# A forward and backward pass in one kernel: the forward tiles of the GLU stage one step earlier, the first weight gradients inside its last tiles

## The chip, the cores and the metric

The kernel runs on one core of a Trainium2 chip. A core has a matrix engine (TensorE, PE in the profile; its weight loads are the row PEld), VectorE (DVE), ScalarE (ACT), GpSimd (POOL) and SyncE (SP). Each engine runs its own instructions in program order and waits on semaphores for the others. Transfers are issued here by SP and GpSimd and carried by 16 DMA engines. The metric is the device time of one execution in microseconds, lower is better; runs of the kernel before: median 537.85 us of 11, from 533.74 to 543.94.

## What is computed

The reference is a residual block and its gradients with respect to nine inputs. S = 2048 rows, D = 512 columns, F = 1376 hidden columns, all bf16.

```python
def _B_ref(x, w_gate, w_up, w_down):
    g = jnp.einsum("bsd,df->bsf", x, w_gate)
    u = jnp.einsum("bsd,df->bsf", x, w_up)
    h = _sigmoid(g) * u
    return jnp.einsum("bsf,fd->bsd", h, w_down)

x = A_q
xn = _layernorm(x, axis=-1)
s = _A_ref(xn, A_k, A_v, A_shift_k, A_ssm_k, A_ssm_D)
g = _silu(_B_ref(xn, B_w_gate, B_w_up, B_w_down))
return x + s * g
```

`_A_ref` is a short shift convolution of k, a product with v, a convolution over the whole sequence length by FFT, and a product with q (here `xn`). The kernel returns the output and the gradients: of x, k, v, the shift weights, the long filter, its skip weight, and the three GLU weights.

## The kernel before

The kernel does not issue its instructions as it is written. Python generators ("streams") record operations in a list; `run_streams` picks the next stream by its progress against a share; `Rec.order` then sorts all recorded operations into one order per engine, by its own cost estimates, looking at most 700 operations ahead; `Rec.emit` (L512) issues them. That is why every row of the profile names L512, and why every tile is called `slab` or `psum`: SBUF is one slab that `Arena` and `Ring` cut up. A record of the trace is assigned to a function by counting: an engine runs in program order, and the counts agree engine by engine (5417 weight loads in the trace, 5033 matmuls and 384 transposes in the program), so the n-th record is the n-th operation.

The work has three stages. **A** (to about 155 us): FFT of k and of k*v for four channel groups (`strK`, `strV`, `strX`), and beside it the forward of nine of the 16 row tiles (`f_gen`, tiles in `FA`), one tile being 128 rows. **B**, the GLU stage (about 155 to 360 us), `stepB`: for each row tile i

- `f_gen(t)`: 88 matmuls of 128 columns for g and u of a later tile, sigma = sigmoid(g) and h = sigma*u, written to DRAM in feature-major order (`hF_d`); for the first NSP = 6 tiles of `FA`, h and sigma are loaded again by `f_ld`;
- `z_gen(i)`: 11 matmuls of 512 columns, z = h w_down, then a chain on VectorE and ScalarE to `dzA`, the gradient of z, which needs `go` (the tile of `grad_out`, loaded by `b_ld` on GpSimd's queue); `dzA` is transposed by DMA for tiles 1 to 12 and on PE for the others;
- `d_gen(i)`: 44 matmuls of 128 columns for dh, and on VectorE the gradients of u and g (`duT`, `dgT`), stored to `uF_d`, `gF_d` on SP's queue;
- `x_gen(i)`: 22 matmuls of 512 columns with `wuT` and `wgT` (weights transposed by DMA on SP's queue), then the layernorm backward on VectorE and a store.

**C** (to the end): the backward FFT (`frontC`, `backC`) mixed with the weight gradients `dW`: nine jobs, three of h (35 blocks of 16 matmuls in all with those of g and u), each needing its operand as a block `L` of 16 KB per partition, loaded from `hF_d`, `gF_d` or `uF_d` by `ld_L` as four DMA transposes of 512 KB on SP's queue. `dW` and `x_gen`, `z_gen` share two accumulator banks of PSUM.

Which tile is where: `SEQ` is the forward order 15, 13, 11, 9, 7, 5, 0, 1, 2, 3, 4, 6, 8, 10, 12, 14 and `POS[i]` a tile's place in it. In `stepB` (L1215 on) the forward of tile i + LAG (LAG = 3) runs inside step i, so that of tile 14 ends in step 11; the flag `fwd` is set there. The layernormed tile is turned by `f_xt`: on PE for places 0 and 1, by DMA on SP's queue from place 2 on. `sig_r`, `h_r` are rings of four buffers in stage B, `v_r[0]` (the third factor of the gradient of g) of three.

After `fwd` the rings of the forward weights are freed and a first block for `L` is made, after `z15` (z of tile 15 recorded) a second; only then is `ld_L` called, and it loads two jobs at most before the end of B. `dW` is run beside the rest of B with the share 0.9 to 1.8, B itself with an estimated length of 520000:

```python
live = run_streams([(gated(stepB(), "B"), 520000, 0.0, 1.0)], until=lambda: "fwd" in flags)
...
live = run_streams(live + [(dW(), 35 * 8192, 0.9, 1.8)], until=lambda: "B" in flags)
```

A stream's position is start + (end - start) * done / length; the stream that is least far goes next. In C `backC` runs from -0.05 to 0.66 against what is left of `dW` (0 to 1).

Of the kernel before, what the change touches and what calls it, by code (L numbers as in the profile page):

```python
# [23 lines left out]
NJ = 16  # L24
NFB = 11
# [4 lines left out]
LAG = 3  # L30
# [4 lines left out]
FA = [15, 13, 11, 9, 7, 5, 0, 1, 2]  # L35
NSP = len(FA) - LAG
SEQ = FA + [i for i in range(NJ) if i not in FA]
POS = {i: n for n, i in enumerate(SEQ)}
# [54 lines left out]
class Ring:  # L93
# [9 lines left out]
    def next(self):  # L103
        a = self.aps[self.i % len(self.aps)]
        self.i += 1
        return a
# [409 lines left out]
def run_streams(streams, until=None):  # L516

    live = [list(st) + [0.0] * (5 - len(st)) for st in streams]
    while live:
        if until is not None and until():  # L520
            break
        for st in sorted(live, key=lambda s: s[2] + (s[3] - s[2]) * s[4] / s[1]):
            try:
                c = next(st[0])
            except StopIteration:
                live.remove(st)
                break
            if c:
                st[4] += c
                break  # L530
        else:
            raise RuntimeError("all streams blocked")
    return live
# [91 lines left out]
def kernel_impl(ctx, tc, A_q, A_k, A_v, A_shift_k, A_ssm_k, A_ssm_D, B_x, B_w_gate, B_w_up, B_w_down,  # L625
# [15 lines left out]
    ar = Arena(slab, SLAB)  # L641
# [4 lines left out]
    def ps_mm(shape, dt=f32, name=None):  # L646
        return nc.ps(PS["mm"], shape, dt)
# [4 lines left out]
    def ps_tr(shape, dt=bf16, name=None):  # L652
        return nc.ps("tr", shape, dt)
# [19 lines left out]
    sig_r, h_r = Ring(ar, [NFB, 128], n=LAG), Ring(ar, [NFB, 128], n=LAG)  # L673
# [6 lines left out]
    flags = set()  # L680
    v_r = []

    def f_major(eng, dst, c, i, src):
        eng.dma_start(dst[c][i // 4, :, i % 4].rearrange("p (a t) -> p a t", t=128), src)

    def f_x(i):
        T[i]["xq"] = xq_r.next()
        nc.gpsimd.dma_start(T[i]["xq"], qC[:, i, :])
# [17 lines left out]
        nc.scalar.activation(xnA[:, i, :], xj, ACT.Identity, bias=nmr_all[:, i:i + 1], scale=rstd_all[:, i:i + 1])  # L706

    def f_xt(i):
        if POS[i] > 1:
            T[i]["xnT"] = xnT_r.next()  # L710
            nc.sync.dma_start_transpose(T[i]["xnT"], xnA[:, i, :])
            return
        pt = ps_tr([4, 128], name="ps_xnT")
        for db in range(4):
            nc.tensor.transpose(pt[:, db, :], xnA[:, i, db * 128:(db + 1) * 128], ident)
        T[i]["xnT"] = xnT_r.next()
        nc.evac(T[i]["xnT"], pt[:], 512)

    def f_gen(i):
        xnT = T[i]["xnT"]  # L720
        n = POS[i]
        if n + 4 < NJ:
            f_x(SEQ[n + 4])
        sigT, hT = sig_r.next(), h_r.next()
        T[i]["sig"], T[i]["h"] = sigT, hT
        uT = None if PS["wide"] else v_r[0].next()
        T[i]["v"] = uT
        for pi, (f0, nb) in enumerate(FBS):
            if PS["wide"]:
                ps = ps_mm([2, 4, 128], name="psGU")  # L730
                pg, pu = ps[:, 0], ps[:, 1]
            else:
                pg, pu = ps_mm([4, 128], name="psG")[:], ps_mm([4, 128], name="psU")[:]
            for pt_, w in ((pg, wg), (pu, wu)):
                for b in range(nb):
                    for db in range(4):
                        nc.tensor.matmul(pt_[:, b, :], w[:, db, (f0 + b) * 128:(f0 + b + 1) * 128], xnT[:, db, :],
                                         start=(db == 0), stop=(db == 3))
            nc.scalar.activation(sigT[:, f0:f0 + nb, :], pg[:, 0:nb, :], ACT.Sigmoid)
            if uT is None:  # L740
                nc.vector.tensor_tensor(hT[:, f0:f0 + nb, :], pu[:, 0:nb, :], sigT[:, f0:f0 + nb, :], ALU.mult)
            else:
                nc.evac(uT[:, f0:f0 + nb, :], pu[:, 0:nb, :], nb * 128)
            if pi == 1 and n + 2 < NJ:
                f_ln(SEQ[n + 2])
            if pi == (2 if n == 0 else 0) and n + 1 < NJ:
                f_xt(SEQ[n + 1])
            yield nb * 1024
        if uT is not None:
            nc.vector.tensor_tensor(hT, uT, sigT, ALU.mult)  # L750
            nc.vector.tensor_tensor(uT, uT, hT, ALU.subtract)
        for c, (f0, nb) in enumerate(FBS):
            f_major(nc.gpsimd, hF_d, c, i, hT[:, f0:f0 + nb])
        if n < NSP:
            nc.gpsimd.dma_start(sF_d[n].rearrange("p (a t) -> p a t", t=128), sigT)

    def f_ld(i):
        n = POS[i]
        sigT, hT = sig_r.next(), h_r.next()
        T[i]["sig"], T[i]["h"] = sigT, hT  # L760
        for c, (f0, nb) in enumerate(FBS):
            nc.gpsimd.dma_start(hT[:, f0:f0 + nb], hF_d[c][i // 4, :, i % 4].rearrange("p (a t) -> p a t", t=128))
        nc.gpsimd.dma_start(sigT, sF_d[n].rearrange("p (a t) -> p a t", t=128))
# [314 lines left out]
    dh_r = Ring(ar, [4, 128], n=2)  # L1078
    wd, wdT, wgT, wuT = wd_r.ap, wdT_r.ap, wgT_r.ap, wuT_r.ap
    dg_r, du_r = Ring(ar, [NFB, 128], n=2), Ring(ar, [NFB, 128], n=2)  # L1080

    def b_ld(i):
        T[i]["x"], T[i]["go"] = xq2_r.next(), go_r.next()
# [115 lines left out]
    def stepB():  # L1199
        f = f_gen(3)  # L1200
        yield from w_gen()
        z = z_gen(0)
        for g in (f, z, f, z, f, z, f):
            c = next(g, None)
            if c:
                yield c
        for i in range(NJ):
            f = f_gen(i + LAG) if 0 < i < NJ - LAG and i + LAG not in FA else iter(())
            d, x = d_gen(i), x_gen(i)
            z = z_gen(i + 1) if i + 1 < NJ else iter(())  # L1210

            def take(g, n):
                for _ in range(n):
                    c = next(g, None)
                    if c is None:  # L1215
                        return
                    yield c
            yield from take(d, 1)
            yield from take(f, 1)
            yield from take(z, 9)  # L1220
            if i == NJ - 2:
                flags.add("z15")
            if i + 2 < NJ:
                b_ld(i + 2)
            if i + LAG in FA[:NSP]:
                f_ld(i + LAG)
            for _ in range(3):
                yield from take(d, 1)
                yield from take(f, 1)
            yield from take(d, 9)  # L1230
            yield from take(f, 9)
            yield from take(x, 9)
            if i + LAG == SEQ[-1]:
                flags.add("fwd")

    stC = {}
    jobs = [(s, c) for s in range(3) for c in range(3)]
    srcs = (hF_d, gF_d, uF_d)
    CH = [(0, 512), (512, 512), (1024, 352)]
    Lfree = []  # L1240

    def ld_L():
        while Lfree and stC.setdefault("Ln", 0) < (len(jobs) if "B" in flags else 2):
            n, blk = stC["Ln"], Lfree.pop(0)
            stC["Ln"] = n + 1
            s, c = jobs[n]
            f0, w = CH[c]
            nb = -(-w // 128)
            L0 = blk.ap.rearrange("p a b -> p (a b)")[:, 0:NJ * nb * 128].rearrange("p (a b) -> p a b", b=128)
            for q in range(4):  # L1250
                nc.sync.dma_start_transpose(L0[:, 4 * q * nb:4 * (q + 1) * nb, :], srcs[s][c][q].rearrange("p j f -> p (j f)"))
            blk.L0 = L0
            stC["L", n] = blk
# [39 lines left out]
    def frontC():  # L1293
        for cg in range(NG):
            Qg = Qg_r.next()
            yield from step1T(lambda j: y2A[:, j, cg * GW:(cg + 1) * GW], Qg, cg in (1, 3))
            while stC["nY"] < 4 * cg:
                yield 0
            Qf = stC["Qf", cg] = Qf_r.next()
            flipT(Qg, cg in (1, 3), Qf, cg > 1)  # L1300
# [104 lines left out]
    def gated(g, flag):  # L1405
        yield from g
        flags.add(flag)
    live = run_streams([(gated(stepB(), "B"), 520000, 0.0, 1.0)], until=lambda: "fwd" in flags)
    for r in (wg_r, wu_r, xq_r, xnT_r):
        r.free()  # L1410
    Lfree.append(Ring(ar, [NJ, 512]))
    ot_r = Ring(ar, [512], n=3)
    live = run_streams(live, until=lambda: "z15" in flags)
    for r in [wd_r] + list(zw.values()):
        r.free()
    Lfree.append(Ring(ar, [NJ, 512]))
    ld_L()
    live = run_streams(live + [(dW(), 35 * 8192, 0.9, 1.8)], until=lambda: "B" in flags)
    for r in [wdT_r, wgT_r, wuT_r, sig_r, h_r, xq2_r, go_r, dg_r, du_r, wq_r, dh_r,
              dxa_r, dzT_r, dxn_r, u1_r, v_r[0]]:  # L1420
        r.free()
# [23 lines left out]
    for n in range(3):  # L1445
# [1 line left out]
    nc.sync.dma_start(Ci.rearrange("p c j n -> p (c j n)"), Ci_d[:])  # L1447
    ld_L()
    dw = live[0]
    live = run_streams([(dw[0], dw[1] - dw[4], 0.0, 1.0), (frontC(), 4 * 4096, -0.05, 0.5),  # L1450
                        (gated(backC(), "back"), 4 * 34816, -0.05, 0.66)], until=lambda: "back" in flags)
    for r in (KK_r, Qg_r, B2_r, Qf_r, Xc_r, Xw_r, P_r):
        r.free()
    Lfree.append(Ring(ar, [NJ, 512]))
# [63 lines left out]
```

## Time and profile before

| | |
|---|---|
| median of 11 runs | 537.85 us |
| the profiled execution | 538.61 us, of which span 536.8 us |
| PE busy | 497.4 us (93%), 5355 matmul records |
| VectorE busy | 401.9 us (75%) |
| ScalarE busy | 343.3 us (64%) |
| GpSimd busy | 125.3 us (23%) |
| DMA | 113.59 MB, mean 212 GB/s |
| granted clock | 0.986 on average; 0.50 at 43.6 to 50.4, 145.95 to 149.37, 326.86 to 330.27 us |

The page's second part shows the last two of these dips in the row of the clock, which is in slices of 13.4 us; the first line is the share of each slice that PE is busy, in tenths:

```profile
PE   4797899999898999999999997999999999999997
...
PEclk9997999999999999999999998999999999999999
```

A matmul's busy time contains the time to its end, so that neighbours overlap; the pace of PE is read as stretch over count. Times in the timeline are microseconds from the span's start; "[3.12 <-X]" is idle time ahead of an instruction and what ended it. A row with SPq or POOLq is an issue on that engine's queue.

### The profile page before, as it was taken

To read this page: it belongs to the slowest core of one execution; us is meant where nothing else is said; L and a number is where in the kernel's file an instruction comes from. 1 tells how busy PE (TensorE), PEld (TensorE's weight loads), DVE (VectorE), ACT (ScalarE), POOL (GpSimd) and SP (SyncE) were. 2 spreads that over 40 slices of the span, in tenths; PEclk is the share of its full clock that TensorE was granted. 3 is DMA by queue.
4 is the path that set the end of the run, shared out by engine and by line. 5 is a ranking of instruction groups with operands and counts; after the bars stand their busy time and mean duration, and the time that the engine had idled before them with its cause. 6 is when DMAs were issued, how large, how long until landed. Compare 5 with 4: busy or idle time off the path is not lost. (4 is left out here: it accounts for less than half of the span.)

```text
span 536.8 us, 13480 instructions
## 1 busy us (share of the span) xinstructions
PE 497.4 (93%) x5355; PEld 354.9 (66%) x5417; DVE 401.9 (75%) x774; ACT 343.3 (64%) x455; POOL 125.3 (23%) x241
## 2 busy tenths in 40 slices
PE   4797899999898999999999997999999999999997
PEld 2687787898786665677666655655746755676644
DVE  7859899965677799787999887767468487765831
ACT  6899999999853443354444533339857869785511
POOL 5152533445413335242424231000000000000000
PEclk9997999999999999999999998999999999999999
DMA  8977797878999465663649599998999789999953
GB/s 261 251 230 252 214 340 212 262 244 242 197 222 180 150 206 146 181 183 117 191 128 232 114 175 209 245 280 239 241 251 202 210 242 213 278 210 242 197 161 115
DMA packets 175345, 113.59 MB, mean 212 GB/s; under 512 B 116119, under 2 KB 159793, under 8 KB 175026
## 3 DMA queue, kind: packets, MB, share of 16 engines
q1 hardware_dynamic: 163648, 78.83, 61.4%
q0 software_dynamic: 11104, 33.89, 21.4%
q8 instruction: 42, 0.69, 0.6%
q14 instruction: 21, 0.17, 0.1%
q10 hardware_dynamic: 530, 0.01, 0.1%
HBM read 37.65 MB, written 45.72 MB: 155 GB/s over the span
## 5 line engine op out<-in xcount | busy, mean ns | idle before, releaser
L512 PE MATMUL psum<-slab 128*128 128x128 bf16 (+4 forms) x5355 | 497.4, 255 | 35.6 <-ACT slab L512 13.0
L512 PEld LDWEIGHTS <-slab 128*128 128x128 bf16 (+2 forms) x5417 | 354.9, 100 | 177.7 <-DVE slab L512 23.7
L512 DVE TENSOR_TENSOR slab<-slab 128x512 bf16<-128x512 bf16 (+5 forms) x472 | 270.0, 609 | 59.2 <-ACT slab L512 31.5
L512 ACT CAST slab<-psum 128x1024 bf16<-128x1024 f32 (+4 forms) x273 | 221.8, 857 | 108.4 <-PE psum L512 87.1
L512 ACT ACTIVATE slab<-psum 128x512 bf16<-128x512 f32 (+2 forms) x80 | 55.0, 690 | 47.4 <-PE psum L512 45.0
L512 ACT COPY slab<-psum 128x1024 bf16<-128x1024 bf16 (+1 forms) x46 | 45.0, 1019 | 17.9 <-PE psum L512 17.9
L512 ACT ACTIVATE slab<-slab 128x512 bf16<-128x512 bf16 (+2 forms) x53 | 41.8, 798 | 14.7 <-DVE slab L512 14.1
L512 POOL DMA_DIRECT2D out_dram<-slab x32 | 17.7, 552 | 105.0 <-DVE slab L512 105.0
L512 DVE TENSOR_TENSOR slab<-psum,slab 128x512 bf16<-128x512 f32 (+2 forms) x47 | 29.3, 626 | 11.2 <-ACT slab L512 6.5
L512 POOL DMA_DIRECT2D hF_d<-slab x48 | 26.4, 552 | 34.0 <-DVE slab L512 33.3
L512 DVE CAST slab<-psum 128x1024 bf16<-128x1024 f32 (+2 forms) x21 | 23.9, 1139 | 13.5 <-PE psum L512 10.0
L512 DVE SCALAR_TENSOR_TENSOR slab<-slab 128x512 bf16<-128x512 bf16 (+2 forms) x64 | 28.1, 439 | 6.9 <-POOL slab L512 5.7
L512 POOL MEMSET slab<- 128x128 bf16 (+3 forms) x11 | 4.3, 400 | 115.1 <-PE psum L512 114.8
L512 DVE SCALAR_TENSOR_TENSOR slab<-psum,slab 128x512 bf16<-128x512 f32 x16 | 11.0, 689 | 20.8 <-PE psum L512 20.7
L512 POOL DMA_DIRECT2D slab<-in_A_q_dram x29 | 16.2, 558 | 33.1 <-ACT slab L512 18.3
L512 POOL DMA_DIRECT2D KK_d<-slab x32 | 17.5, 548 | 22.2 <-ACT slab L512 19.3
L512 DVE TENSOR_SCALAR slab<-slab 128x1 f32<-128x1 f32 (+9 forms) x54 | 16.5, 326 | 2.1 <-ACT slab L512 1.2
L512 DVE STREAM_TRANSPOSE slab<-slab 128x1024 f32<-128x1024 f32 x8 | 14.2, 1821 | 4.6 <-ACT slab L512 4.6
L512 DVE BATCH_NORM_STATS2 slab<-slab 128x6 f32<-128x512 bf16 x16 | 11.0, 688 | 1.5 <-DMA slab<-in_A_q_dram 1.5
L512 POOL TENSOR_TENSOR slab<-slab 128x1 f32<-128x1 f32 x16 | 9.9, 616 | 9.5 <-DVE slab L512 9.3
L512 POOL DMA_DIRECT2D slab<-in_grad_out_dram x16 | 8.9, 559 | 11.8 <-DMA out_dram<-slab 7.3
L512 POOL DMA_DIRECT2D slab<-hF_d x18 | 9.7, 541 | 5.5 <-PE psum L512 4.3
(20 smaller groups left out, 32.7 us busy)
## 6 DMA issues: line engine op xcount, KB each, us to landing
KK_d<-slab POOLq DMA_DIRECT2D x32, 256.0 KB, 4.1
slab<-KK_d SPq DMA_DIRECT2D x16, 512.0 KB, 4.9
slab<-in_A_v_dram SPq DMA_DIRECT2D x4, 1024.0 KB, 10.5
hF_d<-slab POOLq DMA_DIRECT2D x32, 128.0 KB, 4.0
slab<-slab SPq DMA_DIRECT2D x32, 128.0 KB, 4.8
out_dram<-slab POOLq DMA_DIRECT2D x32, 128.0 KB, 3.0
uF_d<-slab SPq DMA_DIRECT2D x32, 128.0 KB, 2.8
gF_d<-slab SPq DMA_DIRECT2D x32, 128.0 KB, 3.2
```

Source lines behind the costliest of these rows:

```text
L512: getattr(getattr(self.nc, eng), meth)(*[place(v) for v in a], **{x: place(v) for x, v in k.items()})
```

## The change

1. In `stepB` the forward of tile i + LAG + 1 runs inside step i, from i = 0 on, so that of tile 14 ends in step 10, where `fwd` is now set. The reload of stored tiles (`f_ld`) moves behind the tile's `d_gen`.
2. `sig_r`, `h_r` and `v_r[0]` get one more buffer each.
3. Tiles 3, 4 and 6 (places 9 to 11) are turned on PE with a copy out of PSUM, no longer by DMA.
4. `ld_L` is called right after `fwd`, into the first block, and may load three jobs before the end of B.
5. B's length is given as 447000; `dW` beside it has the share 0.92 to 2.2. With the old length B's position ended below 0.9, with the new one it reaches 1.0.
6. In C, `frontC` goes to 0.44 (was 0.5) and `backC` to 0.58 (was 0.66).

```diff
@@ f_xt
-        if POS[i] > 1:
+        if POS[i] > 1 and not 8 < POS[i] < 12:
@@ rings of stage B
     dg_r, du_r = Ring(ar, [NFB, 128], n=2), Ring(ar, [NFB, 128], n=2)
+    for r in (sig_r, h_r, v_r[0]):
+        r.extend(Ring(ar, [NFB, 128]))
@@ stepB
         for i in range(NJ):
-            f = f_gen(i + LAG) if 0 < i < NJ - LAG and i + LAG not in FA else iter(())
+            f = f_gen(i + LAG + 1) if i + LAG + 1 < NJ and i + LAG + 1 not in FA else iter(())
...
-            if i + LAG in FA[:NSP]:
-                f_ld(i + LAG)
             for _ in range(3):
                 yield from take(d, 1)
                 yield from take(f, 1)
             yield from take(d, 9)
+            if i + LAG in FA[:NSP]:
+                f_ld(i + LAG)
             yield from take(f, 9)
             yield from take(x, 9)
-            if i + LAG == SEQ[-1]:
+            if i + LAG + 1 == SEQ[-1]:
                 flags.add("fwd")
@@ ld_L
-        while Lfree and stC.setdefault("Ln", 0) < (len(jobs) if "B" in flags else 2):
+        while Lfree and stC.setdefault("Ln", 0) < (len(jobs) if "B" in flags else 3):
@@ stages
-    live = run_streams([(gated(stepB(), "B"), 520000, 0.0, 1.0)], until=lambda: "fwd" in flags)
+    live = run_streams([(gated(stepB(), "B"), 447000, 0.0, 1.0)], until=lambda: "fwd" in flags)
...
     ot_r = Ring(ar, [512], n=3)
+    ld_L()
     live = run_streams(live, until=lambda: "z15" in flags)
...
-    live = run_streams(live + [(dW(), 35 * 8192, 0.9, 1.8)], until=lambda: "B" in flags)
+    live = run_streams(live + [(dW(), 35 * 8192, 0.92, 2.2)], until=lambda: "B" in flags)
...
-    live = run_streams([(dw[0], dw[1] - dw[4], 0.0, 1.0), (frontC(), 4 * 4096, -0.05, 0.5),
-                        (gated(backC(), "back"), 4 * 34816, -0.05, 0.66)], until=lambda: "back" in flags)
+    live = run_streams([(dw[0], dw[1] - dw[4], 0.0, 1.0), (frontC(), 4 * 4096, -0.05, 0.44),
+                        (gated(backC(), "back"), 4 * 34816, -0.05, 0.58)], until=lambda: "back" in flags)
```

## The prediction

> **What bounds the kernel now.** I read the busy table first: TensorE (PE) is busy 497.4 us of 536.8, so only its idle time and its slow-clock time can be won. Then I cut the span by stage (columns: stretch, length, busy us and instruction count of PE, weight loads, VectorE, ScalarE, GpSimd, then granted clock, DMA share, GB/s).
>
> ```profile
> 137.00:172.60 35.60, 30.63 (x408) 25.90 (x409) 26.09 (x55) 21.44 (x32) 8.47 (x17) 0.95 1.13 207
> 172.60:240.00 67.40, 66.20 (x632) 43.43 (x641) 57.33 (x145) 27.13 (x50) 26.78 (x49) 1.00 0.61 169
> 240.00:300.00 60.00, 59.45 (x593) 40.16 (x599) 51.54 (x130) 24.81 (x45) 19.34 (x36) 1.00 0.63 175
> 300.00:318.00 18.00, 17.80 (x183) 12.28 (x183) 17.28 (x43) 10.44 (x18) 4.90 (x9) 1.00 0.80 132
> 318.00:334.00 16.00, 12.28 (x92) 7.88 (x92) 12.02 (x32) 5.06 (x11) 3.33 (x8) 0.89 0.95 179
> 360.00:510.00 150.00, 145.51 (x1493) 94.53 (x1513) 103.39 (x136) 113.18 (x127) 1.77 (x4) 1.00 0.98 231
> ```
>
> In the GLU stage (about 160 to 360) PE is full except in two places: 5.0 us before 172.6, and 3.7 us after 318, where the clock is also down. VectorE is close behind (17.28 of 18.00 before the hole). The timeline shows what the holes are:
>
> ```profile
> 172.60 5.77 PE L512 MATMUL psum<-slab 128*128 128x512 bf16 x25 [1.85 <-DMA slab<-in_B_w_up_dram]
> ...
> 310.06 0.54 POOL L512 DMA_DIRECT2D slab<-in_grad_out_dram  x1
> ...
> 314.90 11.09 SPq L512 DMA_TRANSPOSE slab<-hF_d  x1
> 323.89 0.42 DVE L512 TENSOR_TENSOR slab<-slab 128x512 bf16<-128x512 bf16 x1 [3.12 <-DMA slab<-in_grad_out_dram]
> 326.42 3.50 PEld L512 LDWEIGHTS <-slab 128*128 128x128 bf16 x37 [3.50 <-DVE slab L512]
> ```
>
> and, cut as above, the stretch behind the last hole:
>
> ```profile
> 326.90:330.30 3.40, 3.18 (x31) 3.12 (x30) 3.30 (x11) 2.02 (x4) 1.08 (x2) 0.50 1.13 282
> ```
>
> At 170.4 PE reaches `x_gen(0)` and waits 2.2 us (1.85 after the weight load) for the last transposed `wuT`. At 310.06 GpSimd issues the load of `go` of tile 14; it releases VectorE only at 323.89, 13.8 us later, while SP's queue spends 11.09 us on the fourth transposed load of h. VectorE stands 3.12 us, the dz chain takes another 2.53 us to the PE transposes at 326.42, PE stands 3.5 us there, of which I count 3.4, and then runs 3.18 us of work at clock 0.50, which costs half of it, 1.6. A third hole (2.5 us at 143.8, SP's swap of the k spectrum) keeps its place and its queue order, and is left alone.
>
> **Edit 1: forward tiles one step earlier.** In the changed order `x_gen(0)` is the 2133rd PE operation, before it was the 2086th. 47 more operations stand ahead of the wait; their price comes from a stretch of 128-column work and one of 512-column work:
>
> ```profile
> 190.80:194.00 3.20, 3.20 (x57) 3.08 (x56) 2.99 (x9) 2.79 (x6) 0.54 (x1) 1.00 0.90 330
> 509.30:522.90 13.60, 13.55 (x64) 6.18 (x64) 4.77 (x4) 2.34 (x4) 0.00 (x0) 1.00 0.57 179
> ```
>
> 3.20/57 = 0.056 us and 13.60/64 = 0.213 us (0.216 below, with the change of tile). So 47 x 0.056 = 2.6 us of work that PE does anyhow now hides the 2.2 us. Bounds: 0 to -2.2. I take -2.2: even if the weights land as late as now, the cover is longer than the wait, and three DMA transposes of x leave SP's queue ahead of or among them. With each tile its three h stores and one load of x move ahead on GpSimd's queue; they keep their number, and the loads of `go` they are moved past are due 10 us later or more. The fifth buffer of sigma and h and the fourth of v only permit the order; they cost no instruction.
>
> **Edit 2: tiles 3, 4 and 6 are turned on PE.** 12 more PE operations, 12 x 0.056 = +0.7 us; three more copies out of PSUM (ScalarE 128x512, 0.59 us each) hide in 137 to 172.6, where ScalarE is busy 21.44 of 35.6; uncovered they would be 1.8. Taken: +0.7; bounds 0.7 to 2.5. No row isolates a transpose; the nearest is the 0.056 of 128-column matmuls, and that pace is what I use. The Trainium skill speaks against it ("TensorE: Matmul & The Clock Gate", Part 4: PE-mode transpose): about 275 ns for a 128x128 transpose within a kernel, by which the term would be +3.3 us and the forecast 535.2.
>
> **Edit 3: what the order does to VectorE.** This is the price. With the f tiles gone earlier, tiles 9 to 13 run without them, and a tile of d, x and z alone has more VectorE than PE work. I counted both between the end of one `x_gen` (which releases VectorE's first `x` operation) and the matmul that needs the last of it, with these rows (busy over count):
>
> ```profile
> L512 DVE TENSOR_TENSOR slab<-slab 128x512 bf16<-128x512 bf16 x240 | 93.4, 422 | 8.7 <-DMA slab<-in_grad_out_dram 3.5
> L512 DVE TENSOR_TENSOR slab<-psum,slab 128x512 bf16<-128x512 f32 x34 | 23.3, 686 | 8.7 <-PE psum L512 4.6 <-ACT slab L512 4.1
> L512 DVE SCALAR_TENSOR_TENSOR slab<-slab 128x512 bf16<-128x512 bf16 x32 | 23.0, 720 | 0.6
> L512 DVE TENSOR_TENSOR slab<-slab 128x1408 bf16<-128x1408 bf16 x23 | 20.4, 889 | 1.0 <-ACT slab L512 0.6
> ```
>
> Changed order, `x_gen(8)` to the wait in `x_gen(12)`: 58 products of 512 at 0.389 (22.6), 4 from PSUM at 0.686 (2.7), 6 of 384 at 10.6/32 = 0.33 (2.0), 4 of 1408 at 0.887 (3.5), 2 scalings of 1408 at 4.8/9 = 0.53 (1.1), 12 x-form operations (8 at 0.72, 4 at 0.69: 8.5), 4 small ones at 0.16 and 8 accumulator reads at 0.08 (1.3): 41.7 us. PE in between: 115 of 512 columns at 0.216, 216 of 128 at 0.056, 8 of 256 at 0.11: 37.8. VectorE is 3.9 over. At the front, `x_gen(1)` to `x_gen(4)`, the same count gives 33.8 against 32.6: 1.2 over. Checked on the order before: `x_gen(0)` to `x_gen(4)` 45.5 against 43.2, 2.3 over, where PE really stood 0.40 + 1.12 = 1.5; `x_gen(10)` to `x_gen(12)` 20.6 against 19.6, 1.0 over, where it stood 0.46 + 0.87 = 1.3. The count errs by about +0.25 on average, so I expect 5.1 - 0.5 = 4.6 us. It replaces 1.5 + 1.3 and 0.5 at `x_gen(10)`, 3.3 us. Taken: +1.3; bounds 0 (the elastic case) to +3.
>
> **Edit 4: h's transposed loads from the moment the f tiles end.** The four loads of block 0 move ahead: the fourth now stands with the start of `x_gen(10)`, not in `x_gen(11)`, and the four of block 1 stay in tile 13. So the stall at tile 14 goes (-3.4) with its half clock (-1.6): -5.0, bounds -5.0 to +8 (below). What is late next is `go` of tile 13: its slot is freed by the store of tile 9's output. In the changed order there are 15.4 us of PE work from that store to the dz transposes of tile 13 (56 operations of 512 columns, 51 others); 2.5 of it is the dz chain, so store plus load may take 12.9. The DMA table's medians are 3.0 (stores to `out_dram`) and 4.2 (loads of `grad_out`), 7.2 together. Before, the cover was 19.2 and store plus load took 303.81 to 323.89, 20.1: 20.1 + 2.5 - 19.2 = 3.4, which is the hole. On SP the second and third load of h stand on both sides of the dz transpose of tile 10, which has 7.5 us until `d_gen(10)`; the rows before are 2.06 and 3.93 us, so it holds. Behind the fourth: the dz transpose of tile 12 and the stores of d(11); dz of 12 has 8.3 us until `d_gen(12)`, enough for a 4 us load and not quite for an 11 us one.
>
> **Edit 5: dW of h between tiles 14 and 15, a third load before the end of B, new shares for C.** Same matmuls, other order: 48 instead of 32 of them before `x_gen(15)` ends or right behind it, 94 instead of 133 after the last of `backC`. In C, PE's waits are short (all in 360 to 510 are below 1 us each, 4.5 us idle together). The PE work between a `step3T` and the `inv3` that needs it is 4.0 to 13.5 us before and 3.4 to 11.2 after; waits appeared where it was below about 5. ScalarE, the fuller of the others (113.18 of 150), does not get ahead of PE in either order. Taken: 0; bounds -1.5 to +2.
>
> **Sum.** -2.2 + 0.7 + 1.3 - 5.0 + 0 = -5.2 us. The profiled execution took 538.61 us (536.8 of span, 1.8 around it), 0.8 above the median of the runs, 537.85; I put the sum on the median: 537.85 - 5.2 = 532.6.
>
> **The rivals.** *VectorE takes over.* For: 51.54 of 60 and 17.28 of 18 busy. If the 5.1 us stand without the 0.5, and two of these waits pull the clock to 0.50 for a window as at 145.95 and 326.9 (1.6 each): 532.6 + 0.5 + 3.2 = 536.3, within 0.5%. Against: the waits come as pieces of about 1 us, and the 2.2 us at 170.4 left the clock at 1.00. Against that in turn: 2.5 us of idle at 143.76 were followed by 0.50. The Trainium skill ("TensorE: Matmul & The Clock Gate", Part 1: The HAM clock gate) asks for a whole idle window of about 3.4 us before the clock falls, by which this rival would be 533.1.
>
> *The stuck load moves to tile 13 (slower).* Place: GpSimd's queue behind SP's fourth transposed load of h. If store plus load take 20.1 us again, PE stands 20.1 + 2.5 - 15.4 = 7.2 us, plus 1.6 of clock: 541.4. It decides from 12.9 us on; from about 16 us the gain is gone, from 19.3 the kernel is slower. For: the cover is 3.8 us shorter, since no f tile stands there, and 352 KB of sigma for tile 13 are issued just ahead. Against: only one load of h (512 KB) falls there, where before three and h's own stores came within 12 us; beside the one at 284.34 the loads landed in 6 us.
>
> *The wait at `x_gen(0)` only shifts* (the weights land later, as f's stores now share the queues): 534.8.
>
> **How the numbers follow.** Forecast 0.56, VectorE 0.15, stuck load 0.20 (two thirds of it slower), shifted wait 0.09 (half each side of the bound). About 0.5%, 2.7 us, is what a measurement can tell from no change. Faster 0.61, same 0.25, slower 0.14. Range: -1.5 of C and -1.3 of VectorE below the forecast give 529.8, taken as 529.5; upward to 540, which leaves the full stuck load out.
>
> **What would show it.** Right: no PE wait on `in_B_w_up` before the first `x_gen`; no VectorE wait over 1 us on `in_grad_out` after 250; clock 1.00 from 150 to the end; several PE waits of 0.5 to 1.5 us on VectorE in the last third of the GLU stage; the first 512-column runs of dW before the last `x_gen`. Wrong: a VectorE wait on a load in tiles 12 to 15, a second 0.50 window, or PE idle in C well above 4.5 us.

## The result, and the profile after

The changed kernel takes 530.62 us (median of 12 runs, 526.02 to 542.31), the kernel before 536.98 (47 runs beside it): ratio 0.9882, 95% interval 0.985 to 0.9915. In two later sets of runs the same kernel stood at 0.9912 (0.9873 to 0.9952) and 0.9885 (0.983 to 0.994). Forecast were 532.6 and a range of 529.5 to 540.

The first profiled execution of the changed kernel took 537.48 us (span 535.7), 6.9 above the median of its runs; two more profiles stand below. Its busy times and clock by stretch (columns as before: stretch, length, busy us and count of PE, weight loads, VectorE, ScalarE, GpSimd, granted clock, DMA share, GB/s):

```profile
168.30:172.70 4.40, 0.51 (x3) 0.04 (x2) 4.33 (x10) 0.28 (x1) 2.14 (x4) 1.00 1.21 237
172.90:176.30 3.40, 3.40 (x9) 1.19 (x8) 1.00 (x4) 0.00 (x0) 1.44 (x3) 0.50 0.97 288
...
300.00:318.00 18.00, 16.92 (x149) 10.68 (x150) 17.27 (x45) 6.13 (x10) 4.62 (x11) 1.00 0.72 173
318.00:334.00 16.00, 15.56 (x115) 8.74 (x116) 15.23 (x41) 7.22 (x13) 2.16 (x4) 1.00 0.59 174
...
360.00:510.00 150.00, 144.31 (x1427) 93.96 (x1445) 103.76 (x125) 110.54 (x122) 1.77 (x4) 0.99 0.95 220
```

The hole at tile 14 is filled (15.56 of 16.00 where it was 12.28), and 300 to 318 has become a stretch in which PE waits a little for VectorE (16.92 of 18.00, it was 17.80; VectorE 17.27). But a hole that the prediction had closed is there and larger: of the 4.4 us ahead of 172.7 PE is busy 0.51, and what follows runs at clock 0.50 for 3.4 us. The timeline of the same execution:

```profile
165.33 4.12 SPq L512 DMA_TRANSPOSE slab<-in_B_w_up_dram  x2
...
172.71 5.52 PE L512 MATMUL psum<-slab 128*128 128x512 bf16 x17 [3.90 <-DMA slab<-in_B_w_up_dram]
...
289.73 8.62 PEld L512 LDWEIGHTS <-slab 128*128 128x128 bf16 x75 [1.26 <-DVE slab L512]
...
298.61 0.54 POOL L512 DMA_DIRECT2D out_dram<-slab  x1 [3.56 <-DVE slab L512]
...
300.59 3.79 SPq L512 DMA_TRANSPOSE slab<-hF_d  x1
302.44 0.54 POOL L512 DMA_DIRECT2D slab<-in_grad_out_dram  x1
...
315.22 0.54 POOL L512 DMA_DIRECT2D slab<-in_grad_out_dram  x1
...
489.91 6.26 PE L512 MATMUL psum<-slab 128*128 128x128 bf16 x45 [2.16 <-ACT slab L512]
```

The wait at `x_gen(0)` is still for the last `wuT`. The store of tile 9's output (298.61) and the load of `go` of tile 13 behind it (302.44) now stand beside SP's fourth load of h (300.59); the load landed at 308.2, and no VectorE instruction waits for `grad_out` any more. The last line is new: a wait in C of 2.16 us by this row, 2.49 from one weight load to the next, again with a half-clock window behind it.

### The profile page after: what moved, and what is told of

Same layout as the page of the kernel before. It is cut to its first block, busy times and chain, and to the rows that moved or that the text cites. A ratio compares the mean times of both kernels' runs of the same rounds, so it can differ in the third digit from the quotient of the medians.

```text
span 535.7 us, 13494 instructions
## 1 busy us (share of the span) xinstructions
PE 497.4 (93%) x5373; PEld 353.5 (66%) x5429; DVE 404.0 (75%) x777; ACT 342.7 (64%) x455; POOL 124.5 (23%) x241
## 4 chain that ended last, share of the span: by engine, by line
PE 52%; DVE 20%; ACT 12%; issue 7%; DMA 4%; SPq 3%; POOL 1%; DVEq 0%; ACTq 0%; POOLq 0%
PE psum L512 52%; DVE slab L512 20%; ACT slab L512 12%; SPq L512 3%; DMA slab<-in_A_q_dram 1%; DMA out_dram<-slab 1%; DMA slab<-in_B_w_up_dram 1%; DMA sF_d<-slab 1%; POOL KK_d L512 0%; POOL slab L512 0%; POOL hF_d L512 0%; POOL ksh_d L512 0%; DVEq L512 0%; ACTq L512 0%; POOLq L512 0%
## 5 line engine op out<-in xcount | busy, mean ns | idle before, releaser
L512 DVE TENSOR_TENSOR slab<-slab 128x512 bf16<-128x512 bf16 (+6 forms) x472 | 268.7, 608 | 50.1 <-ACT slab L512 28.5
L512 ACT CAST slab<-psum 128x1024 bf16<-128x1024 f32 (+3 forms) x270 | 219.7, 860 | 99.1 <-PE psum L512 72.2
L512 ACT COPY slab<-psum 128x1024 bf16<-128x1024 bf16 (+1 forms) x49 | 47.2, 1003 | 13.8 <-PE psum L512 13.8
L512 DVE CAST slab<-psum 128x1024 bf16<-128x1024 f32 (+2 forms) x24 | 27.0, 1126 | 18.7 <-PE psum L512 15.2
L512 POOL DMA_DIRECT2D hF_d<-slab x48 | 26.1, 547 | 30.7 <-DVE slab L512 30.5
```

What stands on the lines that cost most here:

```text
L512: getattr(getattr(self.nc, eng), meth)(*[place(v) for v in a], **{x: place(v) for x, v in k.items()})
```

## The experiments

To compare executions I took, for every weight load, the interval to the next one less the pace of its width at full clock (0.056 us for 128 columns, 0.216 for 512, others in proportion). What is left is time that PE lost to waits and to half clock. Summed by stretch, one profiled execution per row ("before" or "changed" says which PE order the row has in front of C; "at `x_gen(0)`" is the wait and the first few matmuls behind it, so that the rest of a half-clock window falls in the next column; the last column is from the last weight load to the end of the span):

| execution | order | start to 143 | to `x_gen(0)` | at `x_gen(0)` | to `x_gen(8)` | to end of `x_gen(12)` | to end of `x_gen(15)` | C | last load to end | span |
|---|---|---|---|---|---|---|---|---|---|---|
| before | before | 31.9 | 4.4 | 2.0 | 0.8 | 0.9 | 4.7 | 7.1 | 4.3 | 536.8 |
| b_look | before | 31.6 | 3.4 | 2.5 | 2.5 | 0.8 | 1.0 | 7.0 | 4.3 | 533.9 |
| b_early_loads | before | 30.5 | 0.4 | 2.8 | 0.8 | 0.9 | 2.3 | 8.0 | 4.3 | 530.6 |
| b_new_C | before | 30.4 | 0.4 | 3.3 | 2.4 | 0.8 | 1.0 | 7.5 | 4.3 | 531.1 |
| after | changed | 31.7 | 0.2 | 4.5 | 1.3 | 2.7 | -0.1 | 9.1 | 4.9 | 535.7 |
| a_again | changed | 32.6 | 0.1 | 3.5 | 1.0 | 2.7 | -0.1 | 5.6 | 4.7 | 531.6 |
| a_third | changed | 30.1 | 0.1 | 3.6 | 1.2 | 2.7 | -0.1 | 6.9 | 4.4 | 530.4 |
| a_old_C | changed | 31.6 | 0.6 | 1.4 | 0.0 | 2.7 | -0.1 | 5.5 | 7.2 | 530.3 |
| a_old_C_pool | changed | 32.8 | 0.2 | 2.4 | 1.7 | 2.7 | -0.1 | 6.0 | 3.7 | 530.9 |
| a_late_loads | changed | 30.5 | 0.1 | 0.0 | 0.0 | 4.8 | -0.1 | 7.0 | 4.6 | 528.4 |
| a_edits123 | changed | 31.9 | 0.1 | 0.7 | 0.0 | 3.3 | -0.1 | 9.6 | 4.0 | 531.0 |
| a_dma_turn | edit 2 undone | 31.4 | 1.9 | 0.3 | 0.0 | 2.7 | -0.1 | 6.7 | 4.3 | 528.0 |
| a_swap0 | gate first | 31.1 | 1.3 | 0.0 | 0.0 | 2.7 | -0.1 | 5.6 | 4.1 | 526.2 |
| a_swap_pool | gate first | 30.5 | 0.1 | 0.0 | 0.4 | 2.7 | -0.1 | 6.0 | 3.7 | 524.8 |

Some columns repeat to 0.1 us in every execution of one order (to the ends of `x_gen(12)` and `x_gen(15)` after the change): these are waits that the order makes, most of them for VectorE. Others differ from one execution to the next of the same order: these are waits for transfers.

The two columns between `x_gen(8)` and the end of `x_gen(15)` have to be read together, since one kind of wait changes its column with the order. A matmul in the first step of the backward FFT waits for a copy by ScalarE, which itself stands behind VectorE:

```profile
308.78 11.27 PE L512 MATMUL psum<-slab 128*128 128x256 bf16 x88 [0.97 <-ACT slab L512]
308.79 0.85 PEld L512 LDWEIGHTS <-slab 128*128 128x128 bf16 x6 [1.25 <-issue]
```

This is the first profile of the change; the wait, 1.2 us, comes before the end of `x_gen(12)`. In b_look, b_early_loads and b_new_C another matmul of the same step waits 1.2, 1.7 and 1.2 us behind that end. Both columns together are 5.6, 1.8, 3.2 and 1.8 us in the order before and 2.6 in the three profiles of the changed kernel.

### a_again, a_third, b_look: the same two kernels, profiled again

No edit.

> The changed kernel once more, for a second profile of it. The first showed three things that the prediction did not have: the hole at 143.8 gone, the wait at x_gen(0) not hidden but grown to 4.25 us with a half-clock window behind it, and a new wait of 2.5 us at 487 in C, also with a half-clock window. Theory 1: all three belong to the change; then they stand here again at the same places (x_gen(0) at least 3 us, 487 at least 2 us) and the profiled execution is again near 537. Theory 2: the wait at x_gen(0) belongs to the change (PE comes earlier by the hole of 143.8, the weights do not), but its size and the wait at 487 depend on how the transfers fall in that execution; then x_gen(0) shows 2 to 4 us, 487 less than 1 us, and the profile is near 531.

> The changed kernel unchanged, to stand beside the other three on the same chip, and for a third profile: x_gen(0) waits 1 to 4.5 us (two profiles had 4.25 and 3.11), no hole at 143.8, no wait of VectorE over 1 us on grad_out after 250, and no wait over 1.5 us in C if that of 2.5 us at 487 was of that one execution.

> The kernel before once more, for a second profile. The first showed a hole of 2.5 us at 143.8 and the stall of 3.4 us at tile 14, each with a half-clock window; the kernel with the early call alone, whose PE, VectorE and ScalarE orders are those of the kernel before, showed neither and yet had the same median. Theory 1 (both belong to the kernel before): both stand here again, span near 535. Theory 2 (both depend on how the transfers fall in one execution): at least one of them is missing or under 1 us, and other waits stand in their place (VectorE at x_gen(13) and in C).

Measured: a_again 529.56 us, ratio 0.9912 (0.9873 to 0.9952); a_third 530.64, ratio 0.9885 (0.983 to 0.994); b_look 535.67, one run. The wait at `x_gen(0)` is there in both new profiles of the change, 3.11 and 3.30 us. That of a_again (the same view, in the same columns):

```profile
172.40 5.83 PE L512 MATMUL psum<-slab 128*128 128x512 bf16 x19 [2.76 <-DMA slab<-in_B_w_up_dram]
```

The hole at 143.8 is in neither, nor a wait of 2.5 us at 487 (a_third has 1.17 us near there): that size was of the one execution. b_look keeps part of the front (1.65 at 143, 1.54 at 148) and lacks the stall at tile 14 altogether:

```profile
304.58 0.55 POOL L512 DMA_DIRECT2D out_dram<-slab  x1 [5.55 <-DVE slab L512]
...
310.82 0.54 POOL L512 DMA_DIRECT2D slab<-in_grad_out_dram  x1
...
318.59 3.42 SPq L512 DMA_TRANSPOSE slab<-hF_d  x1
...
324.11 9.83 PEld L512 LDWEIGHTS <-slab 128*128 128x128 bf16 x90 [0.41 <-DVE slab L512]
```

The queue order is that of the first profile. But SP's fourth load holds its queue 3.42 us, not 11.09, `go` of tile 14 is in at 316.0, and PE waits 0.41 us where it waited 3.50. From the store of tile 10's output to `go` of tile 14 the four profiles of the old order took 20.0, 11.4, 12.3 and 13.9 us. The stall begins at 16.7, the cover of 19.2 less the dz chain of 2.5. So it stood in one profile of four, the one the prediction was made from.

### a_late_loads, b_early_loads: where the loads of h may begin

```diff
 a_late_loads (from the changed kernel)
     ot_r = Ring(ar, [512], n=3)
-    ld_L()
     live = run_streams(live, until=lambda: "z15" in flags)
 b_early_loads (from the kernel before)
     ot_r = Ring(ar, [512], n=3)
+    ld_L()
     live = run_streams(live, until=lambda: "z15" in flags)
```

> The changed kernel, but the loads of h are allowed only where they were before, after z of tile 15 is recorded. On SP's queue the fourth of block 0 keeps its place in x_gen(10); the first three come 184, 49 and 51 PE operations later, close ahead of it. Theory 1 (the prediction's words for edit 4: the earlier call of ld_L is what takes the load of go of tile 14 out of the way): the stall comes back at tile 13 or 14 and the time is 530.6 + 5.0 = 535.6. Theory 2 (the place of the fourth load decides, and that is set by the last forward tile, edit 1): 530.6 within 1.5, no VectorE wait over 1 us on grad_out after 250.

> The kernel before, with ld_L called right after fwd and nothing else. PE, VectorE and ScalarE keep their order; on SP only the first of the four loads of block 0 moves, 22 PE operations ahead, since the others need the h of the last forward tile. Theory 1 (the call of ld_L removes the stall): 537.0 - 5.0 = 532.0. Theory 2 (the fourth load cannot move without edit 1): 537.0 within 1.5, and the wait of VectorE on go of tile 14 is there again with 2 to 4 us.

Measured: a_late_loads 530.99 us, 0.9942 (0.9904 to 0.9979); b_early_loads 535.32, 0.996 (0.9918 to 1.0002). Both times are those of the second theory: the early call alone does not make the kernel before faster by anything like 5 us, and without it the changed kernel keeps most of its gain. The details were missed twice. In b_early_loads no wait on `go` of tile 14 showed, as in b_look; there VectorE waited 1.17 us for `go` of tile 15. And a_late_loads has the wait that the first theory asked for, at tile 13:

```profile
291.66 0.54 POOL L512 DMA_DIRECT2D out_dram<-slab  x1 [1.39 <-DVE slab L512]
...
298.30 3.49 SPq L512 DMA_TRANSPOSE slab<-hF_d  x1
298.66 0.54 POOL L512 DMA_DIRECT2D slab<-in_grad_out_dram  x1
...
305.77 0.43 DVE L512 TENSOR_TENSOR slab<-slab 128x512 bf16<-128x512 bf16 x1 [1.94 <-DMA slab<-in_grad_out_dram]
...
308.73 1.34 PEld L512 LDWEIGHTS <-slab 128*128 128x128 bf16 x24 [2.15 <-DVE slab L512]
```

Store and load took 291.66 to 305.75, 14.1 us, and PE waits 2.15. In a_edits123 they took 12.6 us and VectorE waited 0.45; in the three profiles of the change 9.6, 9.8 and 10.0, and nothing waited. PE did not wait there at 12.6, so the point from which it waits lies between 12.0 and 12.6, 0.3 to 0.9 below the prediction's 12.9. The early call thus moves the third load of h out of the way of the store; as far as these profiles show, it is insurance for tile 13 and not the cure of tile 14.

### a_edits123: forward tiles, buffers and turns alone

The changed kernel with `ld_L` as in a_late_loads, and

```diff
-(len(jobs) if "B" in flags else 3)
+(len(jobs) if "B" in flags else 2)
-gated(stepB(), "B"), 447000, 0.0, 1.0
+gated(stepB(), "B"), 520000, 0.0, 1.0
-dW(), 35 * 8192, 0.92, 2.2
+dW(), 35 * 8192, 0.9, 1.8
-frontC(), 4 * 4096, -0.05, 0.44 ... backC ... 0.58
+frontC(), 4 * 4096, -0.05, 0.5 ... backC ... 0.66
```

> The changed kernel with the loads of h, the lengths and the shares of B and C as before; what is left of the change are the forward tiles one step earlier, the buffers and the turns on PE. The fourth load of h still stands in x_gen(10), 85 PE operations ahead of before. 31 matmuls of dW stand before the end of x_gen(15) and 133 behind the last of backC, as before (32 and 133). Theory 1 (the prediction: -2.2 + 0.7 + 1.3 - 5.0, and the shares 0): 5 us below the kernel before. Theory 2 (the gain is made in C and its tail by the new shares, as the changed kernel with the old shares of C suggests): within 1.5 us of the kernel before.

Measured: 532.69 us, 0.9944 (0.9899 to 0.9989), 3.0 us below the kernel before with an interval of 0.6 to 5.4. It lies between the two theories: taken at its middle, edits 1 to 3 bring about half of the gain, but the interval reaches from almost nothing to nearly all of it.

### a_old_C, a_old_C_pool, b_new_C: the shares of C

```diff
 a_old_C (from the changed kernel; b_new_C is the reverse on the kernel before)
-(frontC(), 4 * 4096, -0.05, 0.44) ... backC ... 0.58
+(frontC(), 4 * 4096, -0.05, 0.5) ... backC ... 0.66
 a_old_C_pool (a_old_C, and)
-            nc.sync.dma_start(dks[0:112, NJ:NJ + 3, :], dks[1:113, 0:3, :])
-            nc.sync.dma_start(dks[112:127, NJ:NJ + 3, :], dks[113:128, 0:3, :])
+            (nc.gpsimd if cg == 3 else nc.sync).dma_start(dks[0:112, NJ:NJ + 3, :], dks[1:113, 0:3, :])
+            (nc.gpsimd if cg == 3 else nc.sync).dma_start(dks[112:127, NJ:NJ + 3, :], dks[113:128, 0:3, :])
```

> The changed kernel with the shares of C as before (0.5 and 0.66). Theory 1 (the prediction: the shares are worth 0): 530.6 within 1.5. Theory 2 (the new shares bring waits such as the one of 2.5 us at 487 with 1.6 of clock): 4 us faster, 526.5. Theory 3 (the new shares are part of the gain): 532.5 or more.

> The changed kernel with the old shares of C, and the two halo copies of dks of the last channel group issued on GpSimd's queue, no longer on SP's behind the last transposed load. The old shares alone gave 534.14 beside 529.56; there VectorE stood 5.5 us for a halo copy and the store of the gradient of k was issued after the last matmul, 7.2 us from the last matmul to the end where the changed kernel has 4.7. Theory 1 (the shares matter by this tail alone): the tail is 4.0 to 4.7 again and the time within 1.5 us of the changed kernel. Theory 2 (the old shares cost in C itself): still 3 to 5 us above the changed kernel.

> The kernel before with the new shares of C alone (0.44 and 0.58). 171 matmuls of dW stand behind the last of backC, before 133, in the changed kernel 94, in the changed kernel with old shares fewer. Theory 1 (the new shares only keep the gradient of k from ending last where less of dW is left; in the kernel before dW ends last anyway): the same as before within 1.5 us. Theory 2 (the new shares are worth 4 to 5 us by themselves): 4 us faster.

Measured: a_old_C 534.14 us, 1.0002 (0.9967 to 1.0036), the whole gain gone; a_old_C_pool 530.47, 0.9879 (0.9825 to 0.9933), the whole gain back; b_new_C 534.93, 0.9973 (0.9938 to 1.0009), no sure difference. PE loses no more in C with the old shares than with the new (5.5 and 6.0 us against 5.6 to 9.1). The end differs. The last 25 us of a_old_C, first its timeline:

```profile
507.09 5.11 SPq L512 DMA_TRANSPOSE slab<-uF_d  x1
...
513.27 0.90 SPq L512 DMA_DIRECT2D slab<-slab  x1
...
516.11 7.52 DVE L512 TENSOR_TENSOR slab<-slab 128x2048 bf16<-128x2048 bf16 x6 [5.54 <-DMA slab<-slab]
```

and its last stretches:

```profile
523.40:524.40 1.00, 0.20 (x2) 0.00 (x0) 0.23 (x1) 0.45 (x1) 0.00 (x0) 1.00 0.00 0
524.40:526.40 2.00, 0.00 (x0) 0.00 (x0) 0.00 (x0) 0.00 (x0) 0.00 (x0) 1.00 0.68 205
526.40:528.40 2.00, 0.00 (x0) 0.00 (x0) 0.00 (x0) 0.00 (x0) 0.00 (x0) 0.58 1.00 290
```

VectorE stands 5.54 us for a halo copy of `dks`, 15 rows, that SP can only issue at 513.27, behind the last transposed load (5.11 us) and some stores. The six products of the gradient of k then take 7.52 us, and its store, 1 MB, begins when PE has just finished: every engine is idle while the DMA engines move up to 290 GB/s, and the end comes 7.2 us behind the last weight load. With the copies on GpSimd's queue the same kernel has:

```profile
509.61 1.07 POOL L512 DMA_DIRECT2D slab<-slab  x2 [37.36 <-DVE slab L512]
...
514.86 7.50 DVE L512 TENSOR_TENSOR slab<-slab 128x2048 bf16<-128x2048 bf16 x6
```

and 3.7 us to the end. The wait for the halo copy is not peculiar to the old shares: VectorE stands 6.68 us for it in a_again and 10.06 in the kernel before. What differs is when the store of 1 MB is issued, against the last weight load: 0.5 us behind it in a_old_C (523.66), 2.4 ahead of it in a_again (524.48), 6.9 ahead in the kernel before (525.58). That kernel leaves 133 matmuls of dW behind the last of `backC`, which hide all of this (4.3 us to the end, set by dW's own last store); once more of dW has been done in B, fewer are left, and the new shares, with 94, restore part of the cover. The longer tail is 2.3 to 2.8 us of the 4.6 that lie between a_old_C and the changed kernel in the medians of their set; the rest is not found in C, and this profile does not show where it is.

### a_dma_turn: edit 2 undone

```diff
-        if POS[i] > 1 and not 8 < POS[i] < 12:
+        if POS[i] > 1:
```

> The changed kernel with tiles 3, 4 and 6 turned by DMA as before: 12 PE operations fewer, three DMA transposes of x more on SP's queue before x_gen(0). Theory 1 (the prediction: the turns on PE cost 0.7 and bring nothing else): 0.7 us below the changed kernel of the same call, no hole at 143.8. Theory 2 (the x transposes on SP's queue are what held up the swap of the k spectrum and the weights; taking them away is the gain of this change in front of x_gen(0)): hole plus wait at x_gen(0) 1 to 4 us larger than in the profiles of the changed kernel (3.1 to 4.5 and less in three of its variants), time 0.5 to 4 us above it. The Trainium skill's 275 ns for a 128x128 transpose (TensorE: Matmul & The Clock Gate, Part 4) would make this kernel 3.3 us faster.

Measured: 534.06 us, 0.9938 (0.9901 to 0.9974), beside 530.64 and 0.9885 (0.983 to 0.994) for the change itself on the same chip. That is the second theory's time, but the intervals overlap, and the profiled execution, at 529.81 the fastest of its twelve, has 1.9 us lost ahead of `x_gen(0)` and 0.3 at it, not the 1 to 4 us more that this theory asked for. The turns on PE are probably no loss; how much they win stays open. Their price can be read from the profiles directly: the twelve transposes of tiles 3, 4 and 6 follow each other at 0.055 to 0.057 us in all nine profiles that have them, 0.67 us together (one record lasts 0.22 us, but they overlap), and not the 3.3 us worked out above from 275 ns each.

### a_swap0, a_swap_pool: the order of the two sums in x_gen(0)

```diff
 both, from the changed kernel
-        for srcT, wT in ((duT, wuT), (dgT, wgT)):
+        for srcT, wT in (((dgT, wgT), (duT, wuT)) if i == 0 else ((duT, wuT), (dgT, wgT))):
 a_swap_pool: also the halo copies of a_old_C_pool
```

> The changed kernel, but x_gen(0) alone adds up dg and the gate weights first, and du and the up weights after; the up weights are the last to be transposed. Nothing else moves. 11 matmuls of 512 columns, 11 x 0.216 = 2.4 us, then stand ahead of the wait. Theory 1 (the wait at x_gen(0), 4.25 and 3.11 us in two profiles of the changed kernel, is for the last up weights alone and what it costs reaches the end, with its half-clock window): wait 0.7 to 1.9 us and no window at 173, time 2.4 to 4 us below the changed kernel, 525.5 to 527.5. Theory 2 (PE is taken up again by the next wait, on VectorE or a load): the changed kernel's 529.6 to 530.6 within 1.

> The changed kernel with the gate weights first in x_gen(0), and the two halo copies of the last group on GpSimd's queue. Theory 1 (the wait at x_gen(0) with its half-clock window, 3 to 5 us in the profiles of the changed kernel, is won by the order of the two sums; the halo copies move the last big store ahead, 0.4 to 0.8): 2.5 to 4 us below the changed kernel of the same call. Theory 2 (the next wait takes it): within 1 us of it.

Measured: a_swap0 528.18 us, 0.9895 (0.9855 to 0.9935); a_swap_pool 526.98, 0.9831 (0.978 to 0.9882), beside 530.64 for the change in the same set. In a_swap_pool PE passes the place of the wait like this:

```profile
159.72 4.25 SPq L512 DMA_TRANSPOSE slab<-in_B_w_up_dram  x2
...
170.04 4.17 PE L512 MATMUL psum<-slab 128*128 128x512 bf16 x26 [0.20 <-DMA slab<-in_B_w_up_dram]
```

The last up weights land at 169.9, 2.8 us after `x_gen(0)` began (167.1), and the eleven gate matmuls have hidden all but 0.4 of it (the table has this in its next column). In the profile of a_swap0 nothing is lost at `x_gen(0)` either, but there the weights had landed 0.4 us before it began, so that this profile would have had no wait in the other order too. Neither has a half-clock window there. a_swap0 misses its expected 525.5 to 527.5 by 0.7 and its interval is no better than that of the change. a_swap_pool is the fastest kernel of this study, 3.7 us below the change in the medians of the same set, within the 2.5 to 4 expected; its interval still meets that of the change between 0.983 and 0.9882, and no set of runs has a_swap0 beside it, so how much of it the halo copies bring is not shown.

## Why the prediction was right, and where it was not

The sum was -5.2 us; the three sets give -6.3, -4.7 and -6.2 by their ratios. Sign and size hold, but several terms did not come from where the text put them, so that the sum came out in part by luck. Two of the signs named for being right failed: PE waits on `in_B_w_up` ahead of the first `x_gen`, and the clock is at 0.50 behind that wait in each of the three profiles of the changed kernel. No VectorE wait over 1 us on `in_grad_out` came after 250, as forecast.

**Edit 1, -2.2 at `x_gen(0)`: the step failed.** The wait was not hidden. Seven profiles have the order of the change on every engine as far as `x_gen(0)` (after, a_again, a_third, a_old_C, a_old_C_pool, a_late_loads, a_edits123): their waits are 4.25, 3.11, 3.30, 1.60, 2.59, 0 and 0.89 us, on average 2.2, where the four profiles of the old order had 2.20, 2.68, 2.96 and 3.48, on average 2.8. The words that fell are "even if the weights land as late as now, the cover is longer than the wait". It is worth adding 2.6 us of work ahead of a wait only if PE starts that work when it did before, and if the weights do not move. In the first profile PE reached the wait at 168.4, earlier than before (170.4), since the hole at 143.8 was gone, and the weights landed at the old time. Over the seven PE reached it at 168.4 on average, over the four at 167.3: 1.1 us later, not 2.6. `x_gen(0)` started at 170.6 against 170.1. That is near the rival "the wait only shifts", but the landing differs by up to 7 us among executions of one order, so that even these averages are uncertain. (Of the 47 operations, 12 are the turns of edit 2, which PE did not do before; the sum is right all the same, since it charges them there.) a_swap_pool shows what does hide the wait: matmuls that do not need the late operand.

**The hole at 143.8, "keeps its place": failed.** Lost time between 143 and `x_gen(0)` is 0.1 to 0.6 us in the same seven profiles (1.3 in a_swap0) and 4.4, 3.4, 0.4 and 0.4 in the old order. The hole was thus no fixture of the old order either. In the first profile of the change the swap of the k spectrum went out at 138.97 instead of 140.98 with the same issues ahead of it on SP's queue, which only went faster. Whether the change keeps the hole away, or these executions happened to be without it, a_dma_turn leaves open. The three columns from 143 to `x_gen(8)` together average 3.2 us in the seven against 6.4: the front did win, and more than the 2.2 of the sum, but most of it ahead of the wait that the sum priced.

**Edit 2, +0.7: right as a price**, 0.67 measured; as a net effect probably too high, by the time of a_dma_turn.

**Edit 3, +1.3: within its bounds.** From `x_gen(8)` to the end of `x_gen(12)` PE loses 2.7 us in each profile of the change and 0.8 to 0.9 before, +1.8; the waits named, with one further ahead, are 0.73 us in `x_gen(4)`, 1.14 in `x_gen(9)`, 1.24 near `x_gen(11)` and 0.71 in `x_gen(12)`, 3.8 together, where 4.6 were expected. But the 1.24 is the wait of the FFT step, which three of the four profiles of the old order have a column later; without it the price is +0.6. None of these waits pulled the clock down, so the rival "VectorE takes over" did not come.

**Edit 4, -5.0: the size was one execution's.** The stall at tile 14 is in one profile of four of the old order and in none of the ten of the changed one. That is what the mechanism asks for, but one case in four is too few to show that the change removed it. Lost time between the ends of `x_gen(12)` and `x_gen(15)` went to -0.1 in every changed order, from 4.7, 1.0, 2.3 and 1.0: on average 2.3, not 5.0, and the wait of the FFT step is 1.2 to 1.7 of it in the last three. Edits 3 and 4 together come to 3.1 us on average before and 2.6 after; without the profile that the prediction was made from, they come to 2.3 before, and nothing is won. Store and load of `go` of tile 13 took 9.6 to 10.0 us, below the point at which the rival of the stuck load would have begun, and with the loads of h late that rival did show, with 1.94 us. And the fourth load of h can only move because the last forward tile does (edit 1); the earlier call moves the first three.

**Edit 5, 0: right as a sum of two terms that the text did not separate.** More of dW before the end of B uncovers the tail of C, and the new shares cover it again; without them the time was 4.6 us longer (534.14 against 529.56 in one set), and with two small copies moved to another queue the ratio was that of the change again (0.9879 beside 0.9885 in another set). The tail is about half of the 4.6.

**What stays open.** By the table the differences come to -3.2 from 143 to `x_gen(8)`, -0.5 from there to the end of `x_gen(15)`, +0.7 for the turns, and, for the three profiles of the changed kernel against before, b_look and b_early_loads, -0.2 in C and +0.4 at the end: -2.8, while the medians are 6 apart. A profile shows one execution, and these were not typical ones: the profiled executions of the changed kernel (537.48, 533.37, 532.25) were 6.9, 3.8 and 1.6 us above the medians of their runs, those of the old order 0.8 above (538.61) and 0.4, 2.9 and 2.1 below (535.67, 532.39, 532.84). The table thus sets slow draws of the one beside fast draws of the other, by 5 us on average, and cannot divide a gain of 6. Which of the waits are shorter in the executions without a profile, no run shows. Half clock is not the rest, since the runs of both kernels lost about the same to it (3.4 to 4.5 us on average before, 3.0 to 3.4 after, from their mean granted clocks). The runs with parts undone put weight on several parts (early loads 0.9942, turns 0.9938, shares 1.0002), and their intervals are as wide as the effects.

## What to carry to other kernels

A wait for a transfer read in one profile is a draw: before it is priced, see in a second execution whether it is there, and count only what the program order itself makes. Set the time of a profiled execution beside the median of its runs before two profiles are subtracted. Work put ahead of a late operand helps little if the engine arrives earlier for another reason or the operand shifts with it; consuming first what is already there is cheaper. When work is moved ahead of a tail, ask which other chain then ends last, and which small copy on a shared queue that chain stands behind.

## What the hardware showed

The same program, in the same queue order, took 11.4 to 20.0 us for one store and the load behind it, and SP's transposed load of 512 KB that ran beside it held its queue 3.42 us in one execution and 11.09 in another.

The half-clock windows from 140 us to the end of C were all close to 3.4 us long. In the fourteen profiles there are nine, behind waits of PE of 4.25, 3.48, 3.38, 3.30, 3.11, 2.68, 2.59, 2.57 and 2.49 us; a wait of 2.96 and all those of 2.20 and below (the longest 2.20, 2.03 and 1.74) were not followed by one. The Trainium skill ("TensorE: Matmul & The Clock Gate", Part 1: The HAM clock gate) gives a free-running window of about 3.4 us. The length agrees with that and so does the chance in it, but a whole idle window was not needed: 2.5 us of standing PE were enough.
